# Ten row tiles of layer 2 turned by VectorE out of spread quarters, and SwiGLU refills asked for one by one

## Chip, core and metric

One core of a Trainium2 chip runs the whole program. The metric is the device time in microseconds from one launch, as the median of several runs. TensorE (PE) does the matrix products, VectorE (DVE) and ScalarE (ACT) the elementwise work, GpSimd (POOL) elementwise work and gathers, SyncE (SP) issues most DMAs. All of them work beside each other and wait for each other through semaphores.

## What is computed

Two rounds of the same two layers over 2048 rows of 1024 numbers, with the same weights in both rounds, all in float32:

```python
x = x + A(layernorm(x), wqkv, wo)            # softmax attention, 32 heads of 32
x = x + B(layernorm(x), w_r, w_gate, w_up, w_down)
x = x + A(layernorm(x), wqkv, wo)
x = x + B(layernorm(x), w_r, w_gate, w_up, w_down)

def B(x, ...):
    r = x @ w_r
    idx = argsort(-r)[:8]                    # eight rows of the sequence
    y = (silu(x[idx] @ w_gate) * (x[idx] @ w_up)) @ w_down
    return x + scatter(idx, y * sigmoid(r[idx]))
```

The layernorm has no weights of its own: (x - mean) / sqrt(var + 1e-5) for each row.

## The kernel before

A "layer" of the code is one attention with the SwiGLU behind it, so there is a layer 1 (`n` = 0) and a layer 2 (`n` = 1). Each has three stages: the projection of all rows to queries, keys and values (`steps`), the attention over 32 units (`half_step`, `pv_step`), and the output projection with the second layernorm and the choice of the eight rows (`t` loop at L1435 ff.). Layer 1's SwiGLU on eight rows is not run at its end: its weight tiles are streamed through, and its products done in between, during layer 2's projection. The program writes out the order of the instructions by hand; each engine takes its own in that order, and a DMA on SP's queue that has to wait holds all those behind it.

**A product of two float32 operands** is done as three products of rounded parts: every operand is split into a high part (ACT copies it to the rounded type) and a low part (DVE or POOL subtracts). The projection has 96 steps `k`, 24 for each of four chunks `c` of 512 rows. A step of queries or keys (`proj`) is 24 matmuls of 512 columns into one PSUM bank, then a high part `hi` by ACT (L955), a low part `lo` by DVE (L956), two stores by SP, and for keys a difference by POOL with a third store, `kd` (L962). A step of values (`proj_v`) has as many matmuls. Weights come in blocks of 1 MB, one for each two steps: `load_w` asks for one (L812), `split_w` two steps ahead of its use has ACT copy it (L836) and POOL subtract it (L841).

**Rows of the next chunk** are got ready during a chunk, one tile of 128 rows in four steps. In layer 2 tile `t` was loaded by one DMA (`ln_load`), its statistics taken (`ln_stat`, L180 to L185), normalised in place (`ln_norm`, L856), and turned by eight TensorE transposes of 128x128 into PSUM (`ln_tr`, L910), with ACT's copy (L913) and DVE's subtraction (L918) behind them. `at` counts the steps of this: 0 normalises, 2 transposes and loads the tile four further on. Layer 1 does not use TensorE for it: it normalises into a copy whose columns are interleaved, stores that copy to DRAM, loads it back in four quarters (each 32 partitions wide, with rows from all of the tile), and turns it by one VectorE transpose of 32x32 blocks (`ln_turn`, L879), then splits it (L885, L888).

**SwiGLU weights** are tiles `fw` of 1 MB (768 KB in the second half of gate and up) in five buffers. `tick` (L629) first asks for as many tiles as the last step freed (`refill`), then does one step on TensorE (L570 for gate and up, L610 for down). Behind every fourth projection step (`k % 4 == 3`) come four ticks, called a group here. So three of its four refills stand among the ticks and the fourth, by the call at the next step, behind that step's weight load. A group uses the four tiles that were asked for at the group before.

**The second layernorm** of layer 1 writes, next to each row of its result x3, two numbers into `mrd` (the mean, and a scale with which the eight rows chosen can be normalised again). Rows that the choice moves to the end of a part are gathered and scattered by POOL's indirect DMAs in `stage`.

## Time and profile before

| | us |
|---|---|
| median of three runs | 4336.01 (4334.86 to 4338.71) |
| the profiled execution | 4337.11 |
| its span, first to last instruction | 4335.3 |
| layer 2's projection in it | 2098 to 2556 |

The profiled execution has 1.8 us outside its span and lies 1.1 us above the median. TensorE is busy in 99% of the span; the profile counts a matmul from its start to its modelled end, so the share says that TensorE has work at all times, and the pace is read from the starts of neighbouring matmuls. In the rows, a line with `x8` is eight instructions merged, the number in brackets is the engine's idle time before, with what ended it, and `SPq` is the DMA queue of SP.

### The profile page before, as it was taken

To read this page: it belongs to the slowest core of one execution; us is meant where nothing else is said; L and a number is where in the kernel's file an instruction comes from. 1 tells how busy PE (TensorE), PEld (TensorE's weight loads), DVE (VectorE), ACT (ScalarE), POOL (GpSimd) and SP (SyncE) were. 2 spreads that over 40 slices of the span, in tenths; PEclk is the share of its full clock that TensorE was granted. 3 is DMA by queue.
4 is the path that set the end of the run, shared out by engine and by line. 5 is a ranking of instruction groups with operands and counts; after the bars stand their busy time and mean duration, and the time that the engine had idled before them with its cause. 6 is when DMAs were issued, how large, how long until landed. Compare 5 with 4: busy or idle time off the path is not lost.

```text
span 4335.3 us, 75837 instructions
## 1 busy us (share of the span) xinstructions
PE 4302.2 (99%) x28255; PEld 2611.7 (60%) x28255; DVE 3046.5 (70%) x5607; ACT 2885.0 (67%) x3447; POOL 3273.4 (76%) x1367
## 2 busy tenths in 40 slices
PE   9999999999999999999999999999999999999998
PEld 7888755555555555558877787555555555555583
DVE  3322678888888888986522215898888888888863
ACT  3333289999999999970222222999999999999510
POOL 5544479999999999925644443899999999999152
PEclk9999999999999999999999999999999999999999
DMA  6877578999999989868598763989989999998698
GB/s 220 271 238 228 165 180 190 204 201 197 205 200 194 214 188 202 172 175 250 180 333 296 256 220 130 209 187 200 208 190 204 201 199 205 199 194 176 180 275 340
DMA packets 350350, 918.70 MB, mean 212 GB/s; under 512 B 48220, under 2 KB 184924, under 8 KB 293646
## 3 DMA queue, kind: packets, MB, share of 16 engines
q0 software_dynamic: 53312, 384.39, 44.2%
q1 hardware_dynamic: 279358, 490.07, 36.0%
q10 hardware_dynamic: 17312, 39.40, 3.3%
q8 instruction: 222, 3.64, 0.3%
q14 instruction: 146, 1.20, 0.1%
HBM read 395.35 MB, written 134.67 MB: 122 GB/s over the span
## 4 chain that ended last, share of the span: by engine, by line
PE 95%; DMA 2%; DVE 1%; issue 1%; POOL 1%; ACT 0%; SPq 0%; POOLq 0%; ACTq 0%; DVEq 0%
PE pv L1162 23%; PE pre L779 22%; PE st L941 17%; PE st L740 15%; PE pre L1450 7%; PE pre L941 6%; PE st L1209 1%; PE pv L570 1%; PE pre L761 1%; PE pv L941 1%; DMA ord<-rd 0%; DMA wol<-in_B_w_up_dram 0%; PE third L779 0%; PE st L610 0%; PE st L761 0%
## 5 line engine op out<-in xcount | busy, mean ns | idle before, releaser
L1172 POOL TENSOR_TENSOR acc<-acc,P 128x2048 f32<-128x2048 f32 x420 | 2058.7, 4902 | 9.4
L1264 ACT ACTIVATE P<-pre 128x1024 f32<-128x1024 f32 x2016 | 1954.8, 1024 | 17.7 <-PE pre L779 13.8
L747 DVE TENSOR_REDUCE nm<-st 128x1 f32<-128x512 f32 x1920 | 1321.6, 688 | 47.4 <-PE st L740 4.6
L779 PE MATMUL pre<-q,ks 64*128 64x512 f32 (+1 forms) x8064 | 1120.5, 395 | 1.8 <-ACT P L1264 1.8
L1162 PE MATMUL pv<-P,v 128*32 128x512 f32 x8192 | 1086.9, 605 | 0.0
L740 PE MATMUL st<-ks,q 64*128 64x512 f32 x2880 | 872.8, 432 | 0.0
L779 PEld LDWEIGHTS pre<-q,ks 64*128 64x128 f32 (+1 forms) x8064 | 771.3, 186 | 156.5 <-ACT P L1264 28.1
L745 DVE CUSTOM_DVE_ANT_0 first<-st,first 128x512 f32<-128x512 f32 x960 | 664.2, 692 | 238.8 <-PE st L740 231.5
L743 ACT ACTIVATE first<-st 128x512 f32<-128x512 f32 x960 | 574.8, 599 | 184.6 <-PE st L740 97.1
L740 PEld LDWEIGHTS st<-dt,q 64*128 64x128 f32 x960 | 175.5, 183 | 798.0 <-DVE nm L745 731.0
L740 PEld LDWEIGHTS st<-ks,q 64*128 64x128 f32 x2880 | 487.4, 185 | 43.2 <-ACT first L743 0.9
L740 PE MATMUL st<-dt,q 64*128 64x512 f32 x960 | 475.6, 495 | 0.0
L1200 POOL DMA_DIRECT2D P<-P x366 | 374.3, 1023 | 105.5 <-ACT P L1264 39.5
L956 DVE TENSOR_TENSOR lo<-st,hi 128x512 fp32r<-128x512 f32 x128 | 88.4, 691 | 507.7 <-ACT hi L955 503.6
L955 ACT CAST hi<-st 128x512 fp32r<-128x512 f32 x128 | 75.1, 587 | 483.5 <-PE st L941 385.4
L841 POOL TENSOR_TENSOR ohl<-wraw,ord 128x2048 fp32r<-128x2048 f32 (+1 forms) x54 | 223.7, 4147 | 218.2 <-ACT ord L836 200.3
L841 POOL TENSOR_TENSOR wl<-wraw,wh 128x2048 fp32r<-128x2048 f32 (+1 forms) x54 | 224.4, 4158 | 173.2 <-ACT wh L840 138.5
L1162 PEld LDWEIGHTS pv<-P,v 128*32 128x32 f32 x8192 | 163.6, 108 | 264.1 <-issue 257.6
L1172 POOL TENSOR_TENSOR acc<-P 128x2048 f32<-128x2048 f32 x62 | 318.7, 5140 | 0.1
L184 POOL TENSOR_TENSOR rs<-mv,eps_c 128x1 f32<-128x1 f32 x64 | 28.5, 445 | 301.0 <-DVE mv L182 301.0
L1450 PE MATMUL pre<-woh,ohl 128*128 128x512 f32 x960 | 223.7, 390 | 1.6 <-DVE pre L1484 0.9
L1381 ACT CAST ohl<-ord 128x1024 fp32r<-128x1024 f32 x32 | 33.6, 1051 | 271.5 <-DVE ord L1372 95.5
(422 smaller groups left out, 5319.6 us busy)
## 6 DMA issues: line engine op xcount, KB each, us to landing
P<-P POOLq DMA_DIRECT2D x366, 1024.0 KB, 9.5
wraw<-in_A_wqkv_dram SPq DMA_DIRECT2D x96, 1024.0 KB
q<-qh SPq DMA_DIRECT2D x256, 128.0 KB
ks<-kh SPq DMA_DIRECT2D x112, 256.0 KB
fw<-in_B_w_down_dram SPq DMA_DIRECT2D x17, 1024.0 KB
vd<-vn SPq DMA_DIRECT2D x32, 512.0 KB
qh<-hi SPq DMA_DIRECT2D x64, 256.0 KB
ql<-lo SPq DMA_DIRECT2D x64, 256.0 KB
```

What stands on the lines that cost most here:

```text
L740: pe.matmul(p, Q[u][rows, 0, i, qt * 128:(qt + 1) * 128], keys, start=True, stop=True, tile_position=(64 * b, 0))
L743: act.activation(side, ps[jj], AF.Relu)
L745: dve.tensor_tensor_reduce(side, ps[jj], side, 1.0, -3.0e38, OP.add, OP.max, NM[u][:, 0, h, qt:qt + 1])
L747: dve.tensor_reduce(NM[u][:, 1 + k, h, qt:qt + 1], ps[1 - jj], axis=AX.X, op=OP.max)
L779: pe.matmul(p[:, b * 512:(b + 1) * 512], KS[(u // QC) % 2][rows, i, slot, kt * 128:(kt + 1) * 128], Q[u][rows, slot, i, :], start=(slot == ...
L841: pool.tensor_tensor(wl[:, sl], raw[:, sl], wh[:, sl].bitcast(F32), op=OP.subtract)
L941: pe.matmul(p, *pair(a, l, r), start=(a == 0 and k == 0), stop=(a == KD - 1 and k == 2))
L1162: pe.matmul(PV[u][32 * h:32 * h + 32, :], V[g, kt // 4][:, kt % 4, 32 * h:32 * h + 32], P[s][:, h, :], start=(kt == 0), stop=(kt == NT - 1 ...
L1172: (dve if on_dve else pool).tensor_tensor(o, a, P[u * NT + k].rearrange("p h c -> p (h c)"), op=OP.add)
L1200: pool.dma_start(P[u * NT + a], P[u * NT + b], accum_op=OP.add)
L1264: act.activation(P[s][:, 2 * i:2 * i + 2, :].rearrange("p h c -> p (h c)"), p, AF.Exp, scale=SCALE)
L1450: pe.matmul(p[:, bl], l[:, a, :], r[a][:, bl], start=(k == 0 and a == 0), stop=(k == 2 and a == KD - 1))
```

## The change

1. Ten tiles of layer 2 (4 to 7 and 9 to 14, `SPREAD`) are loaded as four quarter DMAs of 32 partitions (`ln_next`), normalised by four VectorE operations (`ln_norm_spread`) into a second buffer, and turned by `ln_turn` on VectorE. Tiles 0 to 3, 8 and 15 still go through TensorE. A tile is now loaded two tiles ahead instead of four.
2. Statistics of these tiles are not taken again: layer 1 works out the next layernorm's scale from what it has (five more POOL operations for each of its 16 tiles), `mrd` has four numbers a row, and `spread_stats` brings them in with four DMAs for each chunk. One gather and one scatter more in `stage` move them with their rows.
3. The order of the sum over the 1024 inputs changes in layer 2: weight rows are loaded as `(p a)` instead of `(a p)`, and `columns` hands TensorE's transposes every eighth column of a tile, 32 bytes apart, where they read 128 columns in a row. `ln_norm_spread` reads at the same step.
4. `tick` asks for nothing any more; `refill` asks for one tile and stands in every projection step, so a group's four refills go out at the next four steps, the last of them at the start of the very step that the next group follows.

```diff
-            mg = self.mg = tiny([8, 2], "mg")
+            mg = self.mg = tiny([8, 4], "mg")
...
+            self.gather(tm, abi[:, 0:1], mrd)
...
+            self.scatter(abi[:, 1:2], tm, mrd)
...
         def tick(self):
-            self.refill()
-            self.lag = self.step()
+            self.lag += self.step()
 
         def refill(self):
-            for _ in range(self.lag):
+            if self.lag:
+                self.lag -= 1
                 self.load()
-            self.lag = 0
...
+                if n:
+                    w = w.rearrange("(p a) c -> p a c", a=KD)
+                    w = w if wb < 8 else w[:, 4 * h:4 * h + 4]
+                else:
+                    w = w.rearrange("(a p) c -> p a c", p=128)
...
+            SPREAD = [t for t in range(4, NT - 1) if t != CT - 1] if n else []
...
+            def spread_stats(c):
...
+                for q in range(4):
+                    dma(MS[c][32 * q:32 * q + 32, at:at + 4 * len(ts), :], rows)
+
+            def ln_next(t):
+
+                if t not in SPREAD:
+                    return ln_load(t)
+                XT[t] = pr_.tile([128, D], F32, name="xt", bufs=4)
+                rows = place_of(src, t).rearrange("(g r) (q c) -> q r g c", g=4, q=4)
+                for q in range(4):
+                    dma(XT[t][32 * q:32 * q + 32].rearrange("r (g c) -> r g c", g=4), rows[q])
+
+            def ln_norm_spread(t):
+
+                c, i = divmod(t, 4)
+                XN[t] = pr_.tile([128, D], F32, name="xt", bufs=4)
+                for g in range(4):
+                    sl, st = slice(256 * g, 256 * g + 256), MS[c][:, 4 * i + g, :]
+                    dve.tensor_scalar(XN[t][:, sl].rearrange("p (a c) -> p a c", a=KD), XT[t][:, sl].rearrange("p (c a) -> p a c", a=KD),
+                                      st[:, 0:1], st[:, 2:3], op0=OP.subtract, op1=OP.mult)
...
+            def columns(x, a):
+                return x.rearrange("p (c a) -> p a c", a=KD)[:, a] if n else x[:, a * 128:(a + 1) * 128]
...
-                        pe.transpose(p[:, a, :], XT[t][:, (a0 + a) * 128:(a0 + a + 1) * 128], ident)
+                        pe.transpose(p[:, a, :], columns(XT[t], a0 + a), ident)
...
-                    if prev and k % 4 == 0:
-                        prev.refill()
-
+                if prev:
+                    prev.refill()
...
+                if n and (c, b) in ((0, 2), (0, 23), (1, 23)):
+                    spread_stats(1 + c + b // 23)
                 if norm and at % 4 == 0:
-                    ln_stat(t)
-                    (ln_norm if n else ln_norm_split)(t)
+                    if t in SPREAD:
+                        ln_norm_spread(t)
+                    else:
+                        ln_stat(t)
+                        (ln_norm if n else ln_norm_split)(t)
...
                 if norm and n and at % 4 == 2:
-                    ln_tr(t, True)()
-                    if t + 4 < NT - 1:
-                        ln_load(t + 4)
+                    if t in SPREAD:
+                        ln_turn(t)
+                    else:
+                        ln_tr(t, True)()
+                    if t + 2 < NT - 1:
+                        ln_next(t + 2)
...
-                    mr = small.tile([128, 2], F32, name="mr")
+                    mr = small.tile([128, 4], F32, name="mr")
                     pool.tensor_copy(mr[:, 0:1], mv[:, 0:1])
                     pool.tensor_tensor(mr[:, 1:2], rs, one_c, op=OP.add)
+                    if not n:
+                        pool.tensor_tensor(mr[:, 2:3], mr[:, 1:2], mr[:, 1:2], op=OP.mult)
+                        pool.tensor_tensor(mr[:, 2:3], mr[:, 2:3], mv[:, 1:2], op=OP.mult)
+                        pool.tensor_tensor(mr[:, 2:3], mr[:, 2:3], eps_c, op=OP.add)
+                        pool.tensor_tensor(mr[:, 2:3], mr[:, 2:3], mhalf, op=OP.pow)
+                        pool.tensor_copy(mr[:, 3:4], one_c)
```

On SP, in layer 2's first chunk, from the weight load of step 14 to the first refill behind the group that step 15 ends. `xt` is a row tile, `kh`, `kl`, `kd` and `qh`, `ql` are stores of key and query steps, `wraw` a weight block, `fw` a refill. Before:

```order
L108 DMA wraw<-in_A_wqkv_dram 128x8x256
L108 DMA kh_21180<-hi 128x512
L108 DMA kl_21181<-lo 128x512
L108 DMA kd_21183<-diff 128x256
L108 DMA xt<-x_131 128x1024
L108 DMA kh_21180<-hi 128x512
L108 DMA kl_21181<-lo 128x512
L108 DMA kd_21183<-diff 128x256
L240 DMA fw<-in_B_w_up_dram 128x2048 x3
L108 DMA wraw<-in_A_wqkv_dram 128x8x256
L240 DMA fw<-in_B_w_up_dram 128x2048
```

After:

```order
L108 DMA wraw<-in_A_wqkv_dram 128x8x256
L240 DMA fw<-in_B_w_gate_dram 128x2048
L108 DMA kh_21180<-hi 128x512
L108 DMA kl_21181<-lo 128x512
L108 DMA kd_21183<-diff 128x256
L108 DMA xt<-x_130 32x4x256 x4
L240 DMA fw<-in_B_w_gate_dram 128x2048
L108 DMA kh_21180<-hi 128x512
L108 DMA kl_21181<-lo 128x512
L108 DMA kd_21183<-diff 128x256
L108 DMA wraw<-in_A_wqkv_dram 128x8x256
L240 DMA fw<-in_B_w_up_dram 128x2048
```

The burst of refills behind the group is gone; the last refill that this group needs (the second `fw`, gate) now stands behind step 14's three stores and the four quarter loads of tile 7.

On VectorE, at the same place, one tile's norm and turn (tile 5). Before:

```order
L180 BN_STATS bst<-xt 128x6 x2
L182 BN_AGGR mv<-bst 128x2
L856 TENSOR_SCALAR xt<-xt,mv,rs 128x1024
L956 TENSOR_TENSOR lo<-st,hi 128x512 x3
L918 TENSOR_TENSOR xl<-pre,xh 128x8x128
L956 TENSOR_TENSOR lo<-st,hi 128x512
```

After:

```order
L899 TENSOR_SCALAR xt<-xt,ms 128x256 x4
L996 TENSOR_TENSOR lo<-st,hi 128x512 x3
L916 STREAM_TRANSPOSE xt<-xt 128x1024
L925 TENSOR_TENSOR xl<-xt,xh 128x4x128 x2
L996 TENSOR_TENSOR lo<-st,hi 128x512
```

The statistics go, the norm is in four pieces, and a transpose stands ahead of the low parts, which now read SBUF alone instead of PSUM.

On POOL, in layer 1's output projection next to its end: one tile's small operations, what follows, and the low parts of layer 2's first weights (`ohl`). Before:

```order
L1476 COPY mr<-mv 128x1
L1477 TENSOR_TENSOR mr<-rs,one_c 128x1
L1478 TENSOR_TENSOR mr<-mr,mone 128x1
L1479 TENSOR_TENSOR mr<-mr,rs 128x1
L1489 TENSOR_TENSOR x<-x,xn 128x1024
...
L841 TENSOR_TENSOR ohl<-wraw,ord 128x512 x4
```

After:

```order
L1522 COPY mr<-mv 128x1
L1523 TENSOR_TENSOR mr<-rs,one_c 128x1
L1525 TENSOR_TENSOR mr<-mr 128x1
L1526 TENSOR_TENSOR mr<-mr,mv 128x1
L1527 TENSOR_TENSOR mr<-mr,eps_c 128x1
L1528 TENSOR_TENSOR mr<-mr,mhalf 128x1
L1529 COPY mr<-one_c 128x1
L1530 TENSOR_TENSOR mr<-mr,mone 128x1
L1531 TENSOR_TENSOR mr<-mr,rs 128x1
L1542 TENSOR_TENSOR x<-x,xn 128x1024
...
L847 TENSOR_TENSOR ohl<-wraw,ord 128x512 x4
```

Five small operations stand ahead of the sum and of everything behind it.

## Rows read from the trace of the kernel before

**Rows 1.** The page's head and the busy time of the engines over the whole span.

```profile
span 4335.3 us, 75837 instructions
PE 4302.2 (99%) x28255; PEld 2611.7 (60%) x28255; DVE 3046.5 (70%) x5607; ACT 2885.0 (67%) x3447; POOL 3273.4 (76%) x1367
```

**Rows 2.** [...] The first stretch is the whole projection, the second the four groups of its first chunk.

```profile
2098.40:2556.00 457.60, 457.07 (x2240) 350.64 (x2239) 113.90 (x202) 127.36 (x137) 210.86 (x108) 1.00 0.78 267
2178.00:2256.00 78.00, 78.00 (x404) 57.97 (x403) 21.72 (x34) 22.68 (x23) 33.60 (x20) 1.00 0.97 351
```

**Rows 3.** Waits of TensorE in layer 2's projection (2098 to 2556 us), all of them: us in total, times, the longest.

```profile
PE st L910 <- DVE woh L918: 0.5, 1, 0.5
```

**Rows 4.** TensorE in order of time, one row tile's eight transposes (L910) between two projection steps (L941). First column the start, second the us it lasted.

```profile
2192.33 0.39 PE L941 MATMUL st<-woh,ohl 128*128 128x512 f32 x1
2192.56 0.40 PE L941 MATMUL st<-woh,ord 128*128 128x512 f32 x1
2192.79 1.04 PE L910 MATMUL pre<-ident,xt 128*128 128x128 f32 x8
2193.59 0.48 PE L941 MATMUL st<-woh,ord 128*128 128x512 f32 x1
2193.90 0.40 PE L941 MATMUL st<-woh,ohl 128*128 128x512 f32 x1
```

**Rows 5.** The same view behind a group of SwiGLU steps (L570): once without transposes (2176), once with (2282).

```profile
2176.33 0.50 PE L941 MATMUL st<-woh,ord 128*128 128x512 f32 x1
2176.67 0.40 PE L941 MATMUL st<-woh,ohl 128*128 128x512 f32 x1
...
2282.13 1.09 PE L910 MATMUL pre<-ident,xt 128*128 128x128 f32 x8
...
2283.30 0.40 PE L941 MATMUL st<-xh,ohl 128*128 128x512 f32 x1
```

**Rows 6.** Line 910, the transposes: the weight loads that go with them, ns min/median/max, first and last start.

```profile
L910 PEld LDWEIGHTS pre<-ident,xt x96: 138/140/143, 2165.3 to 2511.9; 128*128 128x128 f32 x96
```

**Rows 7.** VectorE by line in layer 2's projection, shapes kept apart: busy us and mean ns, then the idle time before.

```profile
L918 DVE TENSOR_TENSOR xl<-pre,xh 128x1024 fp32r<-128x1024 f32 x8 | 9.8, 1225 | 6.7 <-ACT xh L913 6.7
L856 DVE TENSOR_SCALAR xt<-xt,mv,rs 128x1024 f32<-128x1024 f32 x12 | 9.8, 813 | 29.8 <-POOL rs L185 29.8
L180 DVE BATCH_NORM_STATS2 bst<-xt 128x6 f32<-128x512 f32 x24 | 15.3, 677 | 0.0
```

**Rows 8.** Lines of VectorE elsewhere in the program, ns min/median/max: layer 1's 32x32 block transposes of a row tile (L879) and its low parts (L888, both operands in SBUF), and two reductions by maximum, one that reads 48 numbers per partition at a step of 64 bytes (L787) and one that reads 512 in a row (L747).

```profile
L879 DVE STREAM_TRANSPOSE xt<-xt x12: 1233/1234/1246, 77.5 to 369.5; 128x1024 f32<-128x1024 f32 x12
L888 DVE TENSOR_TENSOR xl<-xt,xh x24: 677/689/3686, 79.4 to 374.7; 128x512 fp32r<-128x512 f32 x24
L787 DVE TENSOR_REDUCE nmc<-nm x60: 195/199/211, 620.0 to 4011.6; 128x16 fp32r<-128x48 f32 x60
L747 DVE TENSOR_REDUCE nm<-st x1920: 678/687/694, 578.1 to 4009.0; 128x1 f32<-128x512 f32 x192
```

**Rows 9.** The timeline around one burst of refills: SP's issues, then the ScalarE copy that waits for the weights asked for in the burst's midst, then POOL behind it.

```profile
2175.76 1.35 SPq L240 DMA_DIRECT2D fw<-in_B_w_gate_dram  x3
2177.17 0.75 SPq L108 DMA_DIRECT2D wraw<-in_A_wqkv_dram  x1
...
2189.21 2.03 ACT L836 CAST ord<-wraw 128x2048 fp32r<-128x2048 f32 x1 [1.04 <-DMA wraw<-in_A_wqkv_dram]
...
2191.32 4.69 POOL L841 TENSOR_TENSOR ohl<-wraw,ord 128x2048 fp32r<-128x2048 f32 x1 [10.61 <-ACT ord L836]
2195.98 0.73 POOL L962 TENSOR_TENSOR diff<-hi 128x256 fp32r<-128x256 f32 x1
```

**Rows 10.** The timeline: SP's last store (kd) of the projection step that stands one before the step a group follows, SP's next issue, and the group's first matmul (L570); once in the first chunk, once in the second; then four row-tile loads issued in a row.

```profile
2196.73 0.32 SPq L108 DMA_DIRECT2D kd<-diff  x1
2197.14 0.38 SPq L108 DMA_DIRECT2D xt<-x  x1
...
2199.22 3.64 PE L570 MATMUL pv<-fw,xs 128*32 128x512 f32 x32
...
2302.26 0.38 SPq L108 DMA_DIRECT2D kd<-diff  x1
...
2304.96 3.63 PE L570 MATMUL pv<-fw,xs 128*32 128x512 f32 x24
...
2075.02 1.74 SPq L108 DMA_DIRECT2D xt<-x  x4
```

**Rows 11.** TensorE at the end of layer 2, where it uses one 1 MB weight tile after another and waits for each.

```profile
4308.58 1.91 PE L602 MATMUL st<-woh,ht 128*32 128x512 f32 x8 [0.61 <-DMA woh<-in_B_w_down_dram]
4311.14 1.91 PE L602 MATMUL st<-woh,ht 128*32 128x512 f32 x8 [0.65 <-DMA woh<-in_B_w_down_dram]
```

**Rows 12.** POOL in layer 1's output projection: two of the small operations of the statistics by line (busy us, mean ns), then the timeline at the handover to layer 2: POOL's last idle time, the low parts of layer 2's first weights (L841), and TensorE's first matmul that reads them.

```profile
L1478 POOL TENSOR_TENSOR mr<-mr,mone 128x1 f32<-128x1 f32 x15 | 11.5, 768 | 1.2
L1479 POOL TENSOR_TENSOR mr<-mr,rs 128x1 f32<-128x1 f32 x15 | 9.7, 645 | 1.2
...
2093.88 0.65 POOL L184 TENSOR_TENSOR rs<-mv,eps_c 128x1 f32<-128x1 f32 x1 [0.58 <-DVE mv L182]
2096.11 5.67 POOL L841 TENSOR_TENSOR ohl<-wraw,ord 128x512 fp32r<-128x512 f32 x4
...
2102.80 1.07 PE L941 MATMUL pre<-ohl,woh 128*128 128x512 f32 x4
```

More of the change, by code (lines that the diff above doesn't have):

```diff
@@ L128, in tile_kernel @@
     pool.memset(mone, -1.0)
-    cons.tile([128, 136], F32, name="pad")
+    cons.tile([128, 60], F32, name="pad")
     lanes = cons.tile([128, 32], F32, name="lanes")
@@ L684, in layer @@
         else:
[L685 removed]
+            mrd = (dram.tile([CUT + 8, 4], F32, name="mra"), dram.tile([S - CUT, 4], F32, name="mrb"))
         right, mid = ExitStack(), ExitStack()
@@ L863, in ln_norm_split @@
                                   XT[t].rearrange("p (a q c) -> p a q c", q=4, a=KD), mv[:, 0:1], rs, op0=OP.subtract, op1=OP.mult)
+            SPREAD = [t for t in range(4, NT - 1) if t != CT - 1] if n else []
+            MS = {}
+            def spread_stats(c):
+                MS[c] = small.tile([128, 16, 4], F32, name="ms", bufs=1)
+                ts = [t for t in range(4 * c, 4 * c + 4) if t in SPREAD]
+                part, base = (prev.mrd[0], 0) if ts[0] < CT else (prev.mrd[1], CUT)
+                rows = part[ts[0] * 128 - base:(ts[-1] + 1) * 128 - base, :].rearrange("(x r) k -> r x k", r=32)
+                at = 4 * (ts[0] - 4 * c)
+                for q in range(4):
[14 more added lines that the diff above has]
+                                      st[:, 0:1], st[:, 2:3], op0=OP.subtract, op1=OP.mult)
             def ln_store(t):
@@ L877, in ln_turn @@
                 xh, xl = chunk(c, i)
-                rows, turned = XT.pop(t), XN.pop(t)
+                rows, turned = (XN.pop(t), XT.pop(t)) if n else (XT.pop(t), XN.pop(t))
                 dve.transpose(turned, rows)
```

14 lines of the change are left out of this document (6 added, 8 removed).

## The prediction, made before the changed kernel ran

> **What bounds the kernel now.** I read the page's first part, then the windows over layer 2's projection, since nearly all of the change lies there, then TensorE's waits in it. [...] It waits there once, for 0.5 us [rows 3]. So two things follow: no wait can be won back there, only work taken off TensorE; and every new wait of TensorE is added to the time in full. VectorE is busy for 113.90 us of the 457.60 and has room. The DMA engines have little in the first chunk: 0.97 busy, at 351 GB/s [rows 2].
>
> **The sum is made against the profiled execution**, 4337.1 us; it lies 1.1 us above the median of 4336.0, which I take off at the end. A difference of 0.2%, 8.7 us, is about what a measurement of this kernel can tell from no change.
>
> **TensorE's transposes.** Ten of sixteen tiles lose eight transposes each. What a tile costs is read from starts. In the first chunk the last matmul ahead of the transposes starts at 2192.56, the second one behind them at 2193.90: 1.34 us for what two matmul starts of 0.23 us (2192.33 to 2192.56) would take without them, so 0.88 us [rows 4]. In the other chunks they follow a group: from the group's end to the second matmul it is 2282.13 to 2283.30, 1.17 us, and without transposes 2176.33 to 2176.67, 0.34 us, so 0.83 us [rows 5]. Four tiles of the first kind and six of the second: 4 x 0.88 + 6 x 0.83 = 8.5 us off. Nothing else of the change takes work from TensorE, so 8.5 us is the most that it can give.
>
> **VectorE, ACT and the statistics.** A tile loses two statistics operations of 677 ns, a norm of 813 and a subtraction of 1225 [rows 7], 3.4 us. It gains a transpose of 1234 and two subtractions of 689 [rows 8], and four norm pieces. I price a piece by the reduction at a 64-byte step: 48 numbers take 199 ns, 512 in a row 687, so 464 numbers more cost 488 ns, 1.05 ns each, and the step costs nothing [rows 8]. A piece of 256 is then 199 + 208 x 1.05 = 0.42 us, four are 1.7 us, and the sum is 4.3 us, 0.9 us more per tile. The bounds are -1 (a piece at a quarter of 813 ns, 0.2 us) and +8 (both subtractions as the slowest of L888, 3686 ns, where POOL's subtractions run beside it). A tile has four steps of 5.5 us for this and its result is needed in the next chunk, so I put it at nothing; past some 10 us more per tile that would end. On ACT one long copy becomes two short ones, hidden by the same slack.
>
> **The refills** are the term that decides. In the old order three of four go out among the ticks, a whole group ahead of use: TensorE never waits for one [rows 3]. In the new order the fourth goes out at the start of the step that its own group follows, and on SP it is queued behind the stores of the step before, the last of which, `kd`, waits for POOL. Let G be the start of the group. In the second chunk `kd` goes out at 2302.26 with G at 2304.96, 2.7 us ahead of G; in the first at 2196.73 with G at 2199.22, 2.5 us [rows 10]. The first chunk's `kd` is held up: ACT waited 1.04 us for a weight block that was asked for behind three refills, POOL's 4.69 us of low parts came behind that, then the difference of 0.73 [rows 9]. In the new order that block goes ahead of its refill, so I use 2.7 us in both.
>
> Behind `kd` the next issue comes 0.41 us later, and four row-tile loads take 1.74 us [rows 10]. So the fourth refill is issued at G - 2.7 + 0.4 + 1.7 = G - 0.6 where four quarters stand ahead of it (two groups of the first chunk, steps 15 and 23), at G - 1.4 where tile 8's two loads do (step 19), and at G - 2.3 in the later chunks, where the tile is loaded behind the group. It is the fourth tile used, at G + 2.7, three quarters into the group's 3.64 us [rows 10].
>
> How long does 1 MB take to land? At the rate of the DMA engines alone, 2.56 us: at the end of layer 2 TensorE uses one 1 MB tile after the other, 4308.58 to 4311.14, and waits for each [rows 11]. From issue to use: three refills and a weight block, 4 MB, issued from 2175.76 on, had landed at 2189.21, 13.4 us, of which 4 x 2.56 = 10.2 is their own rate; 3.2 us are latency and the stores between [rows 9]. So one lands between 2.6 and 5.8 us after its issue; I take the middle, 4.2. Where quarters stand just ahead, half of their 1.3 us (0.5 MB) more, 0.6.
>
> Steps 15 and 23: G - 0.6 + 4.2 + 0.6 = G + 4.2, needed at G + 2.7, so 1.5 us of wait each (0 to 3.1). Step 19: G - 1.4 + 4.2 + 0.3 = G + 3.1, 0.4 us (0 to 2). Later groups: G - 2.3 + 4.2 = G + 1.9, in time, and with 768 KB sooner; by the long end, G + 3.5, they would wait 0.8 each, and there are two or three of 1 MB with a `kd` ahead. I add 3.4 us (0 to 10).
>
> What else SP has: the quarter loads go into buffers that were free two tiles before, so they wait for little; the twelve `ms` loads have up to 512 pieces of 16 bytes each, most of them behind a group's fourth refill, and a delay of the next block by a us or two is hidden by the two steps between a block's load and its split. I put both at nothing; the price if the cover is gone is a wait of the same us, within the bound above.
>
> **POOL in layer 1's output projection.** Five operations of 0.2 to 0.8 us by the neighbours L1478 and L1479 [rows 12], about 2.2 us a tile. POOL sits idle in most tiles there, but not at the handover: the low parts of layer 2's first weights run from 2096.11 to 2101.78 and TensorE reads the first of them at 2102.80 [rows 12]. Moved by 2.2 us, less the idle 0.58, they end at 2103.4. TensorE reads four parts one after the other, the last about 0.7 us after the first, at 2103.5. I add 0.3 us (0 to 1.6). The additional gather and scatter in `stage` are on POOL in places where a wait has 5 us and more to go, so nothing.
>
> **Strided weight loads of TensorE.** Six tiles still go through TensorE, 48 transposes, and their weight load (140 ns [rows 6]) now takes every eighth number. No row shows a strided weight load. The nearest is VectorE's read at 64 bytes, which costs nothing [rows 8], so I take 0; the upper bound is a load of twice the time, 280 ns. Eight transposes start within 0.80 us, one in 0.10 [rows 4]; at one in 0.28 the 48 cost 48 x 0.18 = 8.6 us.
>
> [...]
>
> **Sum.** 4337.1 - 8.5 + 3.4 + 0.3 = 4332.3 by the profiled execution; less 1.1 it is 4331 us. The gain is real work taken away, and a good third of it is given back as a wait for refills.
>
> **The rivals.**
> First, the strided weight loads: if each takes 280 ns, the sum is 4331 + 8.6 = 4340 us, slower than before. The place is the 32 transposes at the start of the projection and tiles 8 and 15. It decides from 5 / 48 = 0.10 us more per transpose on, that is from a load of about 0.2 us; beyond 0.39 us it is slower by more than 0.2%. For it: PEld is busy for 350.64 of 457.60 us [rows 2] and a longer load has no room among transposes of 0.10 us. Against it: the VectorE row.
> Second, the refills wait by the long end of the bounds: 3 + 3 + 2 us in the first chunk and 0.8 in two later groups, 10 us: 4337 to 4338 us. For it: the DMA engines' 0.97 in the first chunk. Against it: the burst is gone, so the queue in front of a refill is shorter.
> Third, no refill comes late, as the same DMA engines serve a shorter queue: 4327.6 to 4328 us. For it: 2.6 us as the rate of 1 MB, and a `kd` that may go out sooner. Against it: four quarter loads stand ahead of the refill whatever else goes faster.
> Fourth, the turn on VectorE takes so long beside POOL that a chunk is late: with 8 us more a tile there would still be slack, so a small chance.
>
> **How the numbers follow.** Forecast (waits of 1 to 7 us, loads unpunished) 0.58, 4328 to 4335; first rival 0.16; second 0.10; third 0.13; the fourth and others 0.03. Faster by over 0.2% means under 4327.3: the lower half of the third, and a little of the forecast's edge, 0.11. Slower by over 0.2% means over 4344.7: weight loads of three times the time or more, or those of twice together with long refills, 0.09. The rest, 0.80, is within 0.2%. The range from 4326.5 to 4342 leaves out the tail of the first rival and little else.
>
> **What would show it.** Right: in the profile after, L910's counterpart with 48 transposes in layer 2 instead of 128; TensorE's waits in the projection show DMA `fw` two or three times in the first chunk at the fourth tile of a group, 1 to 2 us each, none or less than 1 us later; the weight loads of transposes still at 140 ns and eight transposes in 0.8 us; norm pieces of about 0.42 us. Wrong: weight loads near 280 ns or more; `fw` waits in nearly every group, or none at all; waits of TensorE for a low part by VectorE, or for the `ohl` parts at the handover by more than a us.

## The result and the profile after

| | median, us | ratio to the kernel before, 95% interval |
|---|---|---|
| kernel before | 4337.77 (6 runs, same chip) | |
| kernel after | 4375.62 (4367.65 to 4378.29, 6 runs) | 1.0087 [1.0076, 1.0097] |

The change makes the kernel 38 us slower. The forecast was 4331 us, with a range up to 4342: a gain of 5 us was expected, and a loss was measured.

The page's head of the profiled execution (4375.72 us), to be set beside [rows 1]:

```profile
span 4373.9 us, 75799 instructions
PE 4306.5 (98%) x28175; PEld 2602.6 (60%) x28175; DVE 3080.0 (70%) x5624; ACT 2886.1 (66%) x3454; POOL 3294.6 (75%) x1431
```

TensorE has 80 instructions fewer and is busy for 4.3 us longer. Both can be true only if it ran slower somewhere, so the stage comes next: windows from the first to the last projection matmul of layer 2. As in [rows 2], a line has the stretch in us and its length; the busy us, with the instructions, of PE, PEld, DVE, ACT and POOL; then the clock granted to TensorE as a share of full speed, the mean busy share of the 16 DMA engines and the GB/s they moved. (The first units of the attention stand between its last matmuls, so that it is longer than the projection of [rows 2].) The kernel before:

```profile
2100.90:2706.50 605.60, 605.44 (x2898) 462.85 (x2897) 183.27 (x279) 160.70 (x169) 268.69 (x129) 1.00 0.71 242
```

The kernel after, the stage and then 80 us in the first chunk (in [rows 2] the clock there was 1.00 and the rate 351 GB/s):

```profile
2100.20:2745.10 644.90, 611.22 (x2819) 459.11 (x2818) 213.61 (x296) 161.63 (x176) 267.05 (x122) 0.97 0.71 227
2180.00:2260.00 80.00, 66.38 (x302) 47.96 (x301) 24.97 (x32) 18.65 (x21) 24.10 (x10) 0.89 0.87 269
```

This row alone gives the account. The stage is 39.3 us longer, all of the difference (the spans differ by 38.6). TensorE does not work in 644.90 - 611.22 = 33.7 us of it, where there were 0.2. And it is busy 5.8 us longer, at a granted clock of 0.97 instead of 1.00 (0.89 in the first chunk, 0.94 in the second, from 2300 to 2380 us). What it waits for, in place of the one row of [rows 3]:

```profile
PE pv L572 <- DMA fw<-in_B_w_up_dram: 21.3, 6, 7.7
PE pv L572 <- DMA fw<-in_B_w_gate_dram: 7.3, 3, 5.4
PE st L612 <- DMA fw<-in_B_w_down_dram: 2.9, 1, 2.9
PE st L981 <- POOL ohl L847: 2.0, 1, 2.0
PE st L950 <- DVE woh L958: 0.5, 1, 0.5
```

31.5 us are for refills `fw` (the first three rows), 2.0 for a weight block's low part. The timeline shows the refills. SP's issues first, then TensorE's groups (L572), steps 15, 19 and 23:

```profile
2194.11 0.32 SPq L108 DMA_DIRECT2D kd<-diff  x1
2194.48 3.03 SPq L108 DMA_DIRECT2D xt<-x  x4
2198.48 0.35 SPq L240 DMA_DIRECT2D fw<-in_B_w_gate_dram  x1
...
2219.45 0.38 SPq L240 DMA_DIRECT2D fw<-in_B_w_up_dram  x1
...
2221.04 0.83 SPq L108 DMA_DIRECT2D wraw<-in_A_wqkv_dram  x1
2221.96 1.16 SPq L240 DMA_DIRECT2D fw<-in_B_w_up_dram  x1
...
2228.56 0.36 SPq L240 DMA_DIRECT2D fw<-in_B_w_up_dram  x1
...
2267.33 0.35 SPq L240 DMA_DIRECT2D fw<-in_B_w_up_dram  x1
...
2196.80 2.78 PE L572 MATMUL pv<-fw,xs 128*32 128x512 f32 x24
2204.99 1.94 PE L572 MATMUL pv<-fw,xs 128*32 128x512 f32 x8 [5.41 <-DMA fw<-in_B_w_gate_dram]
...
2230.01 1.92 PE L572 MATMUL pv<-fw,xs 128*32 128x512 f32 x16
...
2241.22 1.94 PE L572 MATMUL pv<-fw,xs 128*32 128x512 f32 x8 [7.70 <-DMA fw<-in_B_w_up_dram]
...
2267.34 2.78 PE L572 MATMUL pv<-fw,xs 128*32 128x512 f32 x24
2275.82 1.94 PE L572 MATMUL pv<-fw,xs 128*32 128x512 f32 x8 [5.70 <-DMA fw<-in_B_w_up_dram]
```

A tile is eight matmuls in these rows; in each group the fourth waits. Read as in the prediction, with G as the group's start and the end of the wait as the landing (the trace's completions of these three loads, 2204.95, 2241.18 and 2275.78, are the ends of the waits):

| step | issued, forecast | issued, measured | landed after issue, forecast | measured | wait, forecast | measured |
|---|---|---|---|---|---|---|
| 15 | G - 0.6 | G + 1.7 | 4.8 | 6.5 | 1.5 | 5.4 |
| 19 | G - 1.4 | G - 1.5 | 4.5 | 12.7 | 0.4 | 0.5 + 7.7 |
| 23 | G - 0.6 | G | 4.8 | 8.5 | 1.5 | 5.7 |

The third tile of step 19 waited too, 0.5 us. Later groups wait another 12.2 us in all, where the forecast had none.

The other terms. The transposes that still go through TensorE (weight loads as in [rows 6], then the place that answers to [rows 5]):

```profile
L950 PEld LDWEIGHTS pre<-ident,xt x16: 185/193/206, 2306.1 to 2550.9; 128*128 128x128 f32 x16
...
2306.14 1.16 PE L950 MATMUL pre<-ident,xt 128*128 128x128 f32 x8
...
2307.37 0.39 PE L981 MATMUL st<-xh,ohl 128*128 128x512 f32 x1
```

A strided weight load takes 193 ns instead of 140, but from the first transpose to the second matmul behind the eight there are 1.23 us instead of 1.17, so 0.06 us for eight. VectorE's lines (busy us, mean ns), to be set beside [rows 7, 8]:

```profile
L899 DVE TENSOR_SCALAR xt<-xt,ms 128x256 f32<-128x256 f32 x40 | 39.3, 1048 | 0.1
L916 DVE STREAM_TRANSPOSE xt<-xt 128x1024 f32<-128x1024 f32 x10 | 12.3, 1228 | 0.0
```

Transpose and subtraction (689 ns) cost what [rows 8] said. The norm pieces take 1.05 us in the mean, not 0.42; the last section comes back to them.

### The profile page after: what moved, and what is told of

Its sections match the earlier page's. It is cut to its first block, busy times and chain, and to the rows that moved or that the text cites. A ratio compares the mean times of both kernels' runs of the same rounds, so it can differ in the third digit from the quotient of the medians.

```text
span 4373.9 us, 75799 instructions
## 1 busy us (share of the span) xinstructions
PE 4306.5 (98%) x28175; PEld 2602.6 (60%) x28175; DVE 3080.0 (70%) x5624; ACT 2886.1 (66%) x3454; POOL 3294.6 (75%) x1431
## 4 chain that ended last, share of the span: by engine, by line
PE 94%; DMA 3%; issue 1%; DVE 1%; POOL 1%; ACT 1%; SPq 0%; POOLq 0%; DVEq 0%; ACTq 0%
PE pv L1208 23%; PE pre L780 22%; PE st L981 17%; PE st L741 15%; PE pre L1496 7%; PE pre L981 6%; PE st L1255 1%; DMA fw<-in_B_w_up_dram 1%; PE pre L762 1%; PE pv L981 1%; DMA fw<-in_B_w_gate_dram 0%; PE pv L572 0%; POOL ohl L847 0%; PE third L780 0%; DMA x<-out_dram,ab 0%
## 5 line engine op out<-in xcount | busy, mean ns | idle before, releaser
L847 POOL TENSOR_TENSOR ohl<-wraw,ord 128x2048 fp32r<-128x2048 f32 (+1 forms) x54 | 223.8, 4150 | 232.5 <-ACT ord L842 216.2
L847 POOL TENSOR_TENSOR wl<-wraw,wh 128x2048 fp32r<-128x2048 f32 (+1 forms) x54 | 224.2, 4154 | 175.6 <-ACT wh L846 137.9
```

Source lines behind the costliest of these rows:

```text
L847: pool.tensor_tensor(wl[:, sl], raw[:, sl], wh[:, sl].bitcast(F32), op=OP.subtract)
```

## The experiments

Theory: the refills asked for one by one land too late, and everything else of the change is worth what the prediction said. Rivals: the quarter loads hold SP or the DMA engines; the strided loads or the turn cost TensorE; the lost clock is a cause of its own. Each run is told by its median and ratio, and by the stage row of its profile as above. Ratios are to be compared, not medians: the kernel before, measured anew beside each set of runs, took 4336.9 to 4340.1 us. "Waits" is the stage less TensorE's busy time; "slower" is the busy time over that of a run without waits (605.5 us with the old tiles, 596.9 with the new, from the last row).

| kernel | us | ratio | stage | waits | slower |
|---|---|---|---|---|---|
| before | | | 605.6 | 0.2 | 0 |
| after | 4375.6 | 1.0087 [1.0076, 1.0097] | 644.9 | 33.7 | 14.3 |
| e1 old refills | 4335.9 | 0.9995 [0.9985, 1.0004] | 602.5 | 2.9 | 2.7 |
| e2 new refills alone | 4368.7 | 1.0071 [1.0056, 1.0087] | 636.2 | 20.8 | 9.9 |
| e3 two by two | 4333.4 | 0.9987 [0.9978, 0.9996] | 601.5 | 2.4 | 2.2 |
| e4 refills on ACT | 4360.8 | 1.0051 [1.0033, 1.0070] | 622.9 | 17.6 | 8.4 |
| e5 quarters on ACT | 4387.5 | 1.0106 [1.0091, 1.0122] | 656.4 | 41.3 | 18.2 |
| e6 filled | 4380.5 | 1.0089 [1.0074, 1.0105] | 643.2 | 20.2 | 9.2 (+16.9 of fill) |
| e7 a step earlier | 4343.6 | 1.0005 [0.9996, 1.0015] | 610.7 | 8.5 | 5.3 |
| e8 quarters behind | 4334.3 | 0.9987 [0.9978, 0.9996] | 600.7 | 2.0 | 1.8 |
| e9 turn early | 4330.5 | 0.9981 [0.9972, 0.9990] | 596.9 | 0.0 | 0 |
| e10 whole rows | 4375.1 | 1.0087 [1.0072, 1.0103] | 642.6 | 31.2 | 14.5 |
| e11 before, two by two | 4339.5 | 1.0005 [0.9996, 1.0014] | 605.6 | 0.1 | 0 |
| e12 half refills | 4368.3 | 1.0067 [1.0051, 1.0084] | 629.8 | 22.3 | 10.6 |

### The two halves of the change, apart (e1, e2)

e1 is the changed kernel with the old asking; e2 the kernel before with the new.

```diff
         def tick(self):
-            self.lag += self.step()
+            self.refill()
+            self.lag = self.step()

         def refill(self):
-            if self.lag:
-                self.lag -= 1
+            for _ in range(self.lag):
                 self.load()
+            self.lag = 0
...
-                if prev:
-                    prev.refill()
+                    if prev and k % 4 == 0:
+                        prev.refill()
```

> The changed kernel with the old asking order of the refills: three among the ticks of a group, the fourth behind the next step's weight load. All else of the change stays (ten turned tiles, quarter loads, four numbers a row). Theory 1, the late refills are the whole loss (31.5 us of waits for fw in the trace, and about 13 us of slower TensorE behind them): no wait for fw is left, granted clock 1.00 in the projection, and the time is before less the transposes, 4329 to 4333 us. Theory 2, the quarter loads and the statistics loads on SP cost by themselves (they hold up stores and weight blocks): the time stays above 4345 us, with waits for other things than fw. Theory 3, the strided weight loads cost: a loss of 3 to 9 us against theory 1, 4334 to 4340 us, with no waits.

> The kernel before with the new asking order of the refills alone, one at each of the next four steps; tiles are still turned by TensorE and loaded by one DMA. Theory 1, asking one by one is too late whatever stands in the queue: waits for fw in most groups, 20 to 30 us in sum, and slower than before by 25 to 45 us, 4362 to 4382 us. Theory 2, the four quarter loads ahead of the fourth refill make it late: waits for fw only of 0 to 2 us a group, under 10 us in sum, 4336 to 4348 us.

No group of e1 waits for a refill, and the 38 us are gone. e2 has 20.6 us of waits for `fw` and most of the loss. So the loss is the asking's. The time of e1, 4335.9 us, is above theory 1's range and within that of theory 3, the strided loads; but its stage has 2.9 us of waits, most of them for weight blocks' low parts, and when those are gone (e9, below) nothing is left for the strided loads to explain. Two things were left: e1 gains 3.1 us in the stage instead of 8.5, and waits are longer with the new tiles than with the old (33.7 and 20.8).

### The hour of asking (e3, e7)

e3 asks for two at each of the two steps behind a group; e7 for two, one and one at the three steps behind it, so that its last goes out a step, 5.4 us, sooner than in the change.

```diff
-                if prev:
+                if prev and k % 4 < 2:
+                    prev.refill()
                     prev.refill()
```

```diff
-                if prev:
-                    prev.refill()
+                if prev and k % 4 < 3:
+                    for _ in range(1 + (k % 4 == 0)):
+                        prev.refill()
```

> The changed kernel with two refills at each of the two steps behind a group instead of one at each of four, so that the last is asked for two steps (11 us) before the group's own step ends. Theory 1, what counts is how long before its use the last refill is asked for: no waits for fw, 4328 to 4334 us. Rival, the sum of the loads does not fit into a group's 26 us when they are interleaved with weight blocks and stores (270 GB/s in the trace after where before had 351): waits for fw remain, over 8 us in sum, above 4342 us.

> The changed kernel with two refills at the first step behind a group and one at each of the next two, so that the last is asked for one step (5.5 us) sooner; turned tiles as in the change. Theory A (only the hour of the last refill decides): it goes out at about 4 us ahead of the group instead of 1.7 us behind its start, lands by G + 2.5, TensorE waits 0 to 1 us three times; 4332 to 4337. Theory B (single loads between small transfers are too slow wherever they stand): waits of 2 us or more stay in several groups; 4345 to 4365.

e3 has no wait for `fw` in a group. In e7 one step takes away all but 6.5 us, mostly here (SP's last issue, then TensorE at step 19):

```profile
2217.67 4.61 SPq L240 DMA_DIRECT2D fw<-in_B_w_up_dram  x1
...
2224.44 2.78 PE L572 MATMUL pv<-fw,xs 128*32 128x512 f32 x24
2231.48 1.93 PE L572 MATMUL pv<-fw,xs 128*32 128x512 f32 x8 [4.25 <-DMA fw<-in_B_w_up_dram]
```

Asked for 6.8 us ahead of the group, this refill is used 13.8 us after its issue. So the hour decides whether TensorE waits, as theory A has it, but the time a load takes is far from the 4.2 us of the forecast and not the same twice, and e7's 4343.6 us lie between the two theories' ranges. The other wait that is left, 2.2 us, is at step 35; the last section comes back to both.

### What makes a late load late (e4, e5, e10, e12)

e4 issues the refills from ScalarE's queue, e5 the quarter loads; e10 loads a spread tile by one DMA of whole rows; e12 loads half of each refill of the first chunk.

```diff
-                    prev.refill()
+                    prev.refill(act)
```

```diff
-                    dma(XT[t][32 * q:32 * q + 32].rearrange("r (g c) -> r g c", g=4), rows[q])
+                    act.dma_start(XT[t][32 * q:32 * q + 32].rearrange("r (g c) -> r g c", g=4), rows[q])
```

```diff
-                for q in range(4):
-                    dma(XT[t][32 * q:32 * q + 32].rearrange("r (g c) -> r g c", g=4), rows[q])
+                dma(XT[t], place_of(src, t))
```

```diff
+                if self.half:
+                    w = w[:, 0:1024]
+                    self.halved.add(u)
                 eng.dma_start(t[:, 0:w.shape[1]], w)
...
                 if prev:
+                    prev.half = k < 28
                     prev.refill()
```

> The changed kernel with its refills issued from ACT's queue, at the same steps. Theory 1a, SP's issue is what is late (a DMA there waits for the one eight places ahead to land, and the fourth refill went out at G + 1.7 in the first late group instead of G - 0.6): issued by ACT it goes out at about G - 1, and waits shrink to 1 to 3 us in the first chunk's groups, 4335 to 4350 us. Theory 1b, the load itself is what is slow (a lone 1 MB took about 5 us from its first packet to its last, in a burst 2.8): waits stay at 3 to 6 us in each of these groups, 4355 to 4375 us.

> The changed kernel (4375.6 us) with the quarter loads of the spread tiles issued from ScalarE's queue instead of SP's; the refills stay one by one. Theory A (the fourth refill is issued late because it is queued behind the four quarter loads, which take 3 us of SP's queue): at steps 15 and 23 it goes out some 3 us sooner, so TensorE's waits of 5.4 and 5.7 us there fall to 2 to 3 us, the others stay; 4366 to 4370. Theory B (asked one by one, a refill lands late in any place, because the load itself is slow beside small transfers): waits of 5 us and more stay at steps 15, 19 and 23; 4372 to 4378.

> The changed kernel (4375.6 us) with each spread tile loaded by one DMA of 128 whole rows instead of four quarter loads; refills one by one, the turn on VectorE as in the change. The rows then lie in another order than the turn wants, so the projected rows are not the reference's. The old tiles with the new refills took 4368.7 us, the new tiles with the old refills 4335.9: together they would give 4367, and the change takes 9 us more. Theory J (these come from the quarter loads: four issues, and pieces of 1 KB in the queue ahead of a refill): 4358 to 4366, TensorE's waits for refills 18 to 22 us instead of 31.5. Rival K (the quarters do not matter; less work on TensorE only makes it wait longer for the same refills): 4370 to 4376, waits of 28 us or more.

> The changed kernel (4375.6 us), still one refill at each step, but the sixteen refills asked for in the first chunk (steps 12 to 27) load half of their columns, 0.5 MB, and TensorE reads that half twice, so its work is the same and the SwiGLU's result another. Theory S (the DMA engines pace the stretch: from the group of step 11 to that of step 27 the kernel before moves 35.2 MB in 105.8 us, 333 GB/s, the changed one 34.4 MB in 130.4 us, 264 GB/s; refills asked late leave engines unused behind a group and are queued behind other loads ahead of the next): with 8 MB less, 26.4 MB, even 264 GB/s is done in 100 us, less than TensorE's 102.2; the waits of 5.4, 8.2 and 5.7 us fall below 1 us each; 4345 to 4355, since later groups keep theirs. Rival R (the time of one lone load decides, its own transfer at 2.56 us for 1 MB): only half of 2.56 us is saved at each, waits of 4 to 7 us stay; 4368 to 4374.

e4: the first chunk keeps waits of 4.7, 3.3 and 5.9 us, the later groups lose theirs but for 0.6 us. So later on SP's queue was what held a refill. In the first chunk it was so at step 19 at most (8.2 us in the changed kernel); the fourth refills of these three steps went out 2.3 to 2.8 us ahead of their groups and were used 8.8 to 11.0 us after their issue, so what is left of the waits there is not SP's. e5 is worse than the change, and no run tells why; 4.5 us of its waits are of TensorE's transposes for VectorE. Its fourth refill of step 15 is asked for 0.4 us behind the group's start instead of 1.7, but is used 8.6 us after that instead of 6.5: asked sooner, there no sooner. Theory A of e5 falls. e10: waits of 31.2 us and the same time as the change, so the quarter loads are not the cause, neither their issues nor their pieces. Rival K's time and waits came out; its reason, less work on TensorE, is not shown by this run, and the last section has another. e12, the fourth tile of steps 15 and 19:

```profile
2203.23 1.32 PE L577 MATMUL pv<-fw,xs 128*32 128x512 f32 x8 [2.59 <-DMA fw<-in_B_w_gate_dram]
2234.66 1.94 PE L577 MATMUL pv<-fw,xs 128*32 128x512 f32 x8 [4.11 <-DMA fw<-in_B_w_up_dram]
```

With 7.3 MB less to move (911.5 MB by the profile's page instead of 918.8; the theory counted 8), waits of 2.6, 4.1 and 2.0 us (step 23) remain where theory S had under 1; S falls: it is not the whole stretch's bytes against the engines' rate. But halving the refills saved 2.8, 4.1 and 3.7 us of wait, more than the 1.3 us of the load's own transfer; so rival R falls too, though the time, 4368.3 us, is in its range. What is left is the queue in front, whose refills are halved with it. The changed kernel's trace shows this queue. Rows as for the stage: from the second refill of steps 15, 19 and 23 to the use of the fourth, and ahead of the second of them a stretch behind the group:

```profile
2182.40:2205.00 22.60, 17.19 (x90) 12.28 (x88) 4.52 (x6) 4.84 (x6) 6.13 (x3) 0.95 0.97 298
2214.00:2219.40 5.40, 5.40 (x25) 4.46 (x25) 5.01 (x3) 0.55 (x2) 3.69 (x1) 1.00 0.13 49
2219.45:2241.22 21.77, 13.56 (x72) 9.03 (x71) 6.23 (x10) 6.48 (x7) 10.07 (x4) 0.90 1.02 306
2252.40:2275.80 23.40, 17.72 (x91) 12.46 (x89) 5.49 (x14) 6.64 (x7) 10.62 (x4) 0.97 0.95 296
```

The DMA engines are 0.95 to 1.02 busy all the while, at 296 to 306 GB/s, and at 0.13 just before step 19's second refill is asked for: SP asks for two stores alone there, and for all the rest behind it. An estimate for step 19: from the refill issued at 2219.45 to the fourth at 2228.56 SP asks for three refills and a weight block of 1 MB each, five stores of 1.2 MB together and 0.5 MB of row tile, 5.9 million bytes by their shapes. With one store issued just before them and two behind, 0.8 million, these are 6.7 million, what 306 GB/s move in 21.8 us. By the trace's completions the fourth refills landed 3.0, 2.7 and 3.6 us after the row tile asked for ahead of them; the rest of the 6.5, 12.6 and 8.5 us since their issue is the queue.

### The clock (e6)

24 matmuls fill TensorE's time ahead of the fourth tile at steps 15, 19 and 23.

```diff
                     for j in range(4):
+                        if j == 3 and k in (15, 19, 23):
+                            spare = ps_pre()
+                            for _ in range(24):
+                                pe.matmul(spare[:, 0:128], ident, ident, start=True, stop=True)
```

> The changed kernel with 24 matmuls of 128x128 whose products nobody uses, on TensorE ahead of the fourth SwiGLU tile at steps 15, 19 and 23, where it waits 5 to 8 us for a refill. Theory C (part of the loss, some 13 us, comes after the waits: TensorE's granted clock falls to 0.89 to 0.94 between 2180 and 2380 us because it stood still): with the waits partly filled the granted clock stays at 0.98 or more there, the time falls to 4362 to 4370, though work was added. Theory D (the clock has nothing to do with the waits, or the fill is too short): clock as before, 4374 to 4382.

The stage, the first chunk as above, and the filling matmuls by line:

```profile
2101.10:2744.30 643.20, 622.99 (x2964) 473.07 (x2962) 213.50 (x296) 161.63 (x176) 267.02 (x122) 0.99 0.71 228
2180.00:2260.00 80.00, 76.06 (x405) 59.00 (x404) 24.87 (x32) 18.76 (x21) 24.87 (x10) 0.98 0.88 276
```

```profile
L1152 PE MATMUL pre<-ident 128*128 128x128 f32 x144 | 16.9, 277 | 0.0
```

The clock of the first chunk comes back from 0.89 to 0.98, and the kernel's own matmuls take 622.99 - 16.9 = 606.1 us instead of 611.22. So the low clock comes from the waits, as theory C has it. In the changed kernel it stands at 1.00 ahead of step 19's group (2214.00 to 2219.40 in the rows above), where matmuls of 512 columns start 0.23 us apart. Right behind that group's wait of 7.7 us it is at half of that, 0.50, and they start 0.43 us apart:

```profile
2241.20:2246.00 4.80, 4.78 (x15) 2.56 (x16) 0.00 (x0) 0.00 (x0) 0.54 (x1) 0.50 1.08 299
```

But e6's stage is shorter by 1.7 us only, and the ratio is the same as the change's within the intervals: the fourth tiles are used at 2206.1, 2241.5 and 2274.9 us, in the changed kernel at 2205.0, 2241.2 and 2275.8, and the groups of steps 27 and 31 wait 3.9 us instead of 1.9. In its time theory D is right: this fill does not win back what the clock costs.

### Where the gain of the new tiles was (e8, e9, e11)

e8 is e3 with the quarter loads behind the weight block; e9 is e8 with VectorE's turn at the start of its step; e11 is the kernel before with e3's asking.

```diff
+                if norm and n and at % 4 == 3 and t + 2 < NT - 1:
+                    ln_next(t + 2)
...
-                    if t + 2 < NT - 1:
-                        ln_next(t + 2)
```

```diff
+                if norm and n and at % 4 == 2 and t in SPREAD:
+                    ln_turn(t)
...
-                    if t in SPREAD:
-                        ln_turn(t)
-                    else:
+                    if t not in SPREAD:
                         ln_tr(t, True)()
```

> The best version so far (two refills at each of the two steps behind a group, 4333.4 us) with the quarter loads moved one step later, behind the weight block of the projection instead of ahead of it. Theory E (the gain of 8.5 us on TensorE did not come out whole because a weight block lands late behind the quarter loads, 7.5 us of ScalarE's idle time ahead of its copy and 2.0 us of TensorE's wait for the low part): that wait goes, 4330 to 4332. Rival F (block and quarters share the same DMA engines, so that their order does not matter, or the refill comes late instead): 4333 to 4337.

> The kernel with two refills at each of the two steps behind a group and the quarter loads behind the weight block (4334.3 us in the run before), and now VectorE's turn of a spread tile at the start of its step, ahead of the SwiGLU group, instead of behind it. Theory G (the 2.0 us that TensorE waits for POOL's low part in the second chunk comes from the turn: VectorE's reciprocal of 3.35 us in the group stands ahead of the turn, ScalarE's copies of the turned tile wait 4.5 us for that, and its copy of the weight block is queued behind them): TensorE's wait for ohl goes; 4331 to 4333. Rival H (the weight block is late by its DMA, not by the copy ahead of it): the wait of 2.0 us stays; 4333 to 4336.

> The kernel before, with its refills asked for two at each of the two steps behind a group, and nothing of the tiles changed. Theory L (the gain of the best version over the kernel before is the turned tiles' alone): same as before within 2 us. Rival M (asking two by two is itself worth something over the burst): 3 us or more faster than before. If it is slower by 2 us or more, two by two costs a little too, and the turned tiles bring more than the best version shows.

e8 changes nothing: theory E falls, rival F stands. Its timeline shows the chain, from VectorE over ScalarE and POOL to TensorE:

```profile
2306.17 3.35 DVE L582 RECIPROCAL fy<-fy 96x512 f32<-96x512 f32 x1
2309.44 1.18 DVE L916 STREAM_TRANSPOSE xt<-xt 128x1024 f32<-128x1024 f32 x1
2310.66 1.14 ACT L922 CAST woh<-xt 128x512 fp32r<-128x512 f32 x2 [4.50 <-DVE xt L916]
2311.70 1.91 ACT L842 CAST ord<-wraw 128x2048 fp32r<-128x2048 f32 x1
2313.69 4.58 POOL L847 TENSOR_TENSOR ohl<-wraw,ord 128x2048 fp32r<-128x2048 f32 x1 [2.73 <-ACT ord L842]
2318.32 0.50 PE L981 MATMUL st<-xh,ohl 128*128 128x512 f32 x1 [1.96 <-POOL ohl L847]
```

The turn stands behind the SwiGLU's reciprocal; ScalarE's copy of the turned tile waits 4.50 us for it, with the copy of the weight block queued behind. e9 takes the turn out of this chain, and its stage is the first with nothing left over:

```profile
2101.10:2698.00 596.90, 596.90 (x2820) 454.53 (x2818) 222.33 (x296) 162.12 (x176) 268.73 (x122) 1.00 0.74 245
```

8.7 us shorter than before, at a clock of 1.00. By its times e9 is 0.19% faster than the kernel before, some 8 us; e11 gains nothing, so the turned tiles bring it, with the turn early in its step. e9 is the best version found.

## Why the prediction was wrong, step by step

**TensorE's transposes, -8.5 us: right.** With every wait gone (e9) the stage is 8.7 us shorter, and TensorE's busy time in it 8.5 (605.44 to 596.90).

**The refills, +3.4 us (0 to 10): the step that failed.** The mechanism was named, the place too (the fourth tile, steps 15, 19 and 23), and e1, e3 and e7 show it. The term measured 31.5 us of waits. What was mis-sized is "1 MB lands 2.6 to 5.8 us after its issue": 6.5, 12.7 and 8.5 us were measured. The short end is a rate at which nothing but 1 MB loads is moved [rows 11]; the long end puts 3.2 us of a burst's latency on one load, with nothing in front of it [rows 9]. In the changed kernel a weight block and the third refill were still on their way when step 19's fourth was asked for: by the trace's completions they landed at 2229.92 and 2232.41, and it was issued at 2228.56. At steps 15 and 23 it stood behind three stores and four quarter loads. The sentence against the second rival, that the queue in front of a refill is shorter because the burst is gone, is the error in one line: the same bytes are asked for in the same steps, only later. The second rival had the right term and a bound three times too low. The DMA engines' 0.97 [rows 2] spoke for it and was given too little weight.

The hour of issue was right at step 19 and wrong by 2.3 us at step 15. The four quarter loads took SP 3.03 us instead of 1.74 there, and then the refill waited 0.9 us on SP for an earlier load to land:

```profile
SPq L240 <- DMA fw<-in_B_w_gate_dram: 0.9, 1, 0.9
```

That load is the group's third refill (landed 2198.42; the fourth went out at 2198.48), as at step 23 (2267.27 and 2267.33). So a late landing also made the next issue late. "Later groups: in time" was wrong by the same error, and by SP's queue (e4, and the last section).

**VectorE, 0: wrong.** "A tile has four steps of 5.5 us for this and its result is needed in the next chunk, so I put it at nothing" asks for the tile's own deadline alone. The norm pieces, 1.05 us in the mean instead of 0.42, stand ahead of the low parts of the step, and SP's queue stands behind those (last section). Two workings of this term do not hold either: its upper bound, +8 us, comes to 6.9 by its own rows (0.9 and two subtractions 3.0 us longer each), and two reductions of different length [rows 8] cannot give both the cost of a number and that of the step, though a piece alone did take the 0.43 us.

**No price for the clock: missing.** "Every new wait of TensorE is added to the time in full" is too little here. In the table a wait brings 0.4 to 0.6 us more per us where waits are long (after 14.3 to 33.7, e4 8.4 to 17.6, e7 5.3 to 8.5). Waits and slower matmuls together are 48.0 us (33.7 and 14.3); less the 8.5 of the transposes and the 0.2 of waits before, these are the stage's 39.3.

**Strided weight loads, 0 (rival 1, 280 ns): right in the sum.** The load does get longer, 193 ns instead of 140; by what, no run shows. But the transposes get only 0.06 us longer per eight. Rival 1 needed 0.10 us per transpose.

**The turn on VectorE, 0 (rival 4): wrong by 2 us of wait**, 3.8 us of the stage with the slower matmuls behind it (e8's 600.7 to e9's 596.9). Not because VectorE lacks time; ScalarE's in-order queue carries its lateness to a weight block (in e8 its copy of the turned tile waits 4.50 us, and the block's copy starts behind it, at 2311.70). The prediction looked for who waits for the turned tile, and not for what is queued behind the copy that waits.

**The handover and POOL, +0.3: right in size, not in its working.** From the start of layer 1's last matmul to that of the stage's first it is 2.6 us before and 2.7 after. But nothing was moved by 2.2 us: the low parts run from 2095.97 to 2101.66 (before, 2096.11 to 2101.78), and the last tile's small operations stand behind them on POOL, in both kernels.

**Left open.** The new tiles with the new asking wait 13 us more than the old tiles with it (33.7 and 20.8), though the two times' intervals touch. The quarter loads are not the reason (e10). Of the 10.9 us among them that are for refills, 4.7 are at step 35, behind held norm pieces (last section). That a TensorE with less to do arrives earlier at the same landings may explain some of the rest; no run separates it.

## What to carry to other kernels

Before a prefetch is spread out in time, count what is still in flight ahead of its last piece, and price the landing at the rate of that stretch, not at the rate of a burst or of a lone load; where the DMA engines are 0.97 busy the burst was the buffer. When a step is moved to another engine, look at the in-order queues: what stands behind it on its new engine, behind the copy of its result, and behind the stores that these feed became late too here (4.50 us at ScalarE's copy in e8, 7.7 us at SP's store ahead of step 35's group). Price a wait of TensorE with the clock that it costs afterwards, here 0.4 to 0.6 us for each us of long waits.

## What the hardware showed that was not expected

VectorE's norm pieces (L899) and POOL's low parts (L847) of the changed kernel, in order of time:

```profile
2342.76 4.59 POOL L847 TENSOR_TENSOR ohl<-wraw,ord 128x2048 fp32r<-128x2048 f32 x1 [2.73 <-ACT ord L842]
2347.91 4.71 POOL L847 TENSOR_TENSOR ohl<-wraw,ord 128x2048 fp32r<-128x2048 f32 x1 [0.57 <-ACT ord L842]
...
2343.80 9.54 DVE L899 TENSOR_SCALAR xt<-xt,ms 128x256 f32<-128x256 f32 x4
```

```profile
L899 DVE TENSOR_SCALAR xt<-xt,ms x40: 428/523/4928, 2149.9 to 2515.3; 128x256 f32<-128x256 f32 x40
```

Four pieces of 0.43 us take 9.54 us; POOL's two subtractions end at 2347.35 and 2352.62, and the pieces that are held end up to 0.3 us behind them. A single piece took up to 4.9 us, about the length of one of POOL's.

The tile has time for this, but what stands behind it has not. VectorE's low part for the query step is next in its order, SP waits for that low part, and the refill is behind its store. SP's wait between 2346 and 2354, its issues, and the group of step 35:

```profile
SPq L108 <- DVE lo L996: 7.7, 1, 7.7
...
2345.90 0.32 SPq L108 DMA_DIRECT2D qh<-hi  x1
2353.97 0.32 SPq L108 DMA_DIRECT2D ql<-lo  x1
2355.02 0.66 SPq L240 DMA_DIRECT2D fw<-in_B_w_up_dram  x1
...
2364.50 1.93 PE L572 MATMUL pv<-fw,xs 128*32 128x512 f32 x6 [4.30 <-DMA fw<-in_B_w_up_dram]
2368.34 1.93 PE L572 MATMUL pv<-fw,xs 128*32 128x512 f32 x6 [1.91 <-DMA fw<-in_B_w_up_dram]
```

The two stores of the step go out 8.1 us apart, in e2 (old tiles, same asking) 0.7 us apart at the same place, and this group waits 6.2 us where e2's waits 1.5. The two groups that still wait in e7, steps 19 and 35, are the two whose refills SP held up like this, with waits of 5.9 and 7.7 us for a low part. At step 19 of the changed kernel the hold (7.05 us for four pieces) delays a refill by some 4 us as well, but e2 has as long a gap there, behind POOL's statistics. That the held pieces cost time is thus read from traces; no run takes them out under the new asking.

Eight of the forty pieces took 1.1 to 4.9 us. Each of these ended 0.26 to 0.28 us behind an operation of POOL that had run beside it, seven times a subtraction of L847 and once L583. The other 32 took 0.43 to 0.58 us. What on the chip holds a piece no run shows.
